# One program in five queues: the order of work and 89 engine choices drawn anew, in a kernel of a recurrent attention and a Fourier mixing block

## The chip, the cores and the metric

The kernel runs on one core of one Trainium2 chip. The core has a matrix engine (TensorE, PE in the profile; its weight loads are listed apart as PEld), a vector engine (VectorE, DVE), a scalar engine (ScalarE, ACT), GpSimd (POOL) and SyncE (SP). Each has a queue of its own that it works through in the order in which the program lists it. Data moves between main memory (DRAM) and on-chip memory (SBUF) by DMA. Matmul results land in PSUM, which the program uses as eight banks, each of 512 float32 values per partition.

The metric is the device time of one execution in microseconds (us), less is better. The times shown are medians over several executions.

## The reference

Inputs are r, k, v and w of shape batch 4 x heads 8 x sequence 768 x head size 48, u (8 x 48), and two weight matrices (384 x 1536 and 1536 x 384). First a linear attention with a decaying state:

```python
for t in range(S):
    cur = np.einsum('bhd,bhe->bhde', u[None] * kt, vt)
    y[:, :, t] = np.einsum('bhd,bhde->bhe', rt, state + cur)
    state = wt[:, :, :, None] * state + np.einsum('bhd,bhe->bhde', kt, vt)
```

Then, on x, which is y with its heads side by side (4 x 768 x 384):

```python
X = np.fft.fft(np.fft.fft(x, axis=1), axis=2)
u = x + np.real(X)
un = (u - mean) / np.sqrt(var + 1e-06)      # over the last axis
out = u + np.maximum(un @ w_ch1, 0.0) @ w_ch2
```

The output is float32, 4 x 768 x 384.

## The kernel before

*Tiling.* The four batches are cut into six chunks of 128 time steps each, chunk (b, c). Within a chunk the recurrence is written as matrix products: the logarithms of w are summed up along time by a matmul with a triangular matrix (lines 944 and 948), exponentials of the sums (lines 950 and 963) scale r and k (`rkh`, lines 982 and 985), both are transposed (`rkt`), their product gives a 128 x 128 matrix per head (line 1014) that is masked (line 1019) and multiplied with v (line 1064), and a state of 48 x 48 per head is carried from chunk to chunk (line 1040, its decay at 1048). The term with u is `rk`: r times k (967), times u (969), summed over a head (971), times v (`vtd`, 974). Batch 0 handles its chunks in pairs (`attention2`). For the first two batches the transposes of `rkt` run on TensorE; from chunk 12 on they are DMA transposes that SP issues (line 990).

*Mixing.* The rows of a batch are folded by symmetry (`sd`, `xf`), multiplied with cosine and sine tables (line 1128, results `hcs`, and a reversed copy of them, `hcr`, lines 1137 to 1142), then with a second table (line 1151). The sum with x is `uf` (1153), its statistics follow (1157, 1159), then the centred rows `un` (1163), which are transposed to `unt`, on TensorE for batches 0 and 1 and by DMA (line 1180) for batches 2 and 3. For each half batch (three chunks of 128 rows) twelve products with the first weight matrix (line 1198) are evicted with a ReLU to `ht`, on ACT (line 1205) or DVE (line 1203), and the products with the second one (line 1216) are scaled, added to `uf` on DVE (line 1220) and written out by a DMA that SP issues (line 1224).

*Order.* The program first makes a list of 1439 operations, numbered as they are made, each with its dependencies and the engines that could do it. The dictionary `ORDER` at the head of the file says for each of the five engines which operations it does, and in which order. So an operation that several engines can do runs on the engine under which its number stands. `_Prog.schedule` walks through these lists with fixed cost figures, in which it also decides which PSUM bank a tile gets (the one that is free first by its figures). `_Prog.emit` then writes the instructions and a semaphore wait wherever an operation needs a result of another engine. An engine that waits holds up everything behind it in its own list; SP's list holds all loads, outputs and DMA transposes, except for the two weight matrices, which POOL issues. Instructions whose operands allow more than one engine pass through helpers, so that many have the same line in the profile (533 for products and sums of two tensors, 547 and 556 for ACT, 557 for DVE copies).

*Numbers that the text uses.* The operations below belong to the last chunks of batch 3, its mixing and its last products.

| number | engine | what it does |
|---|---|---|
| 1203, 1202 | SP | load r and k of chunk (3, 4) |
| 1232, 1233 | SP | load k and r of chunk (3, 5) |
| 1011 | SP | DMA transpose of the second half of `un` of batch 2 |
| 1217, 1211, 1212, 1183 | POOL | k part of `rkh` of (3, 4); `rk` of (3, 4) and its product with u; `vtd` of (3, 3) |
| 1192, 1213 | DVE | decay of the state of (3, 3); head sums of `rk` of (3, 4) |
| 1245, 1246 | DVE | r part and k part of `rkh` of (3, 5) |
| 1247, 1248 | SP, PE | DMA transpose of `rkt` of (3, 5); its 128 x 128 products |
| 1336, 1338, ..., 1358 | PE | the twelve first products of half 0 of batch 3, each followed by the number of its eviction (1337, 1339, ...) |
| 1360 to 1407 | PE, DVE, SP | second products, evictions and outputs of batch 3 |
| 1080, 1085, 1090 | DVE | output evictions of half 1 of batch 2 |

Of the kernel before, what the change touches and what calls it, by code (L numbers as in the profile page):

```python
# [35 lines left out]
        "6 1419 1420 1421 1422 1423 1424 1425 86 92 1426 94 1427 1428 1429 78 1430 97 1431 82 113 115 146 1432 1433 "  # L36
        "148 1434 114 128 116 151 1435 1436 80 121 134 202 124 204 1437 167 169 425 1438 168 170 207 127 136 223 "
        "130 175 137 224 225 178 426 428 226 182 183 181 185 186 190 231 192 234 238 193 455 239 457 437 237 454 "
        "254 438 246 241 441 242 255 247 484 256 466 444 257 262 270 271 467 263 258 272 273 486 483 274 470 275 "
        "259 276 277 278 279 280 281 264 265 266 267 513 284 473 302 293 303 304 285 286 495 515 294 496 322 295 "  # L40
        "313 447 314 331 332 323 502 324 476 333 512 315 291 309 547 549 300 525 580 524 356 346 362 352 344 354 "
        "364 499 528 329 360 348 350 320 342 338 358 546 591 397 399 534 579 531 403 401 381 558 505 559 385 590 "
        "383 393 776 778 562 594 366 367 775 376 567 565 389 368 377 395 597 802 804 612 371 604 372 605 801 378 "
        "620 373 621 606 622 613 614 615 623 624 607 625 626 608 609 627 628 629 630 631 616 788 617 387 791 643 "
        "828 634 644 635 645 636 391 830 652 672 653 410 681 654 673 682 854 674 683 856 827 411 641 663 664 665 "
        "405 415 814 650 412 406 817 659 853 885 407 820 416 712 417 679 887 794 702 704 670 688 706 696 843 698 "
        "840 866 714 694 915 700 884 747 872 737 869 753 739 914 692 749 741 743 731 846 726 708 900 897 727 1098 "
        "710 1124 1097 902 926 1126 751 1100 716 936 745 929 944 937 728 733 1150 952 945 953 717 954 938 1152 718 "
        "955 956 946 939 940 957 958 959 960 941 961 947 1176 948 962 963 949 735 973 1123 980 974 721 975 966 967 "
        "981 982 1004 997 968 1005 1113 722 998 765 723 1178 1006 990 999 766 991 992 755 756 760 1110 1136 1139 "  # L50
        "757 767 761 1149 762 1175 1022 1020 1014 1036 1018 1028 1026 1116 1024 1016 1142 1030 1207 1165 1209 1038 "
        "1188 1162 1032 1039 1043 1206 1044 1034 1236 1194 1168 1237 1065 1191 1069 1059 1073 1045 1055 1219 1061 "
        "1053 1222 1048 1248 1224 1075 1057 1067 1274 1251 1040 1063 1049 1266 1071 1267 1275 1077 1258 1259 1276 "
        "1268 1277 1269 1260 1261 1278 1279 1262 1280 1263 1281 1282 1283 1270 1271 1284 1285 1082 1295 1288 1289 "
        "1290 1302 1296 1297 1326 1303 1312 1304 1319 1327 1087 1328 1078 1313 1320 1050 1321 1088 1314 1083 1079 "
        "1084 1089 1338 1342 1344 1350 1340 1348 1358 1354 1336 1356 1391 1389 1393 1377 1397 1387 1383 1346 1352 "
        "1381 1375 1370 1379 1371 1365 1399 1385 1360 1361 1362 1372 1366 1395 1367 1409 1414 1410 1404 1411 1400 "
        "1401 1415 1405 1416 1406"),
    "act": (
        "0 20 21 22 23 24 25 26 91 87 93 103 95 96 79 108 145 98 83 147 117 150 149 118 119 201 162 152 203 81 424 "  # L60
        "206 205 171 427 172 173 208 174 138 157 131 227 229 228 218 213 73 453 429 187 194 458 482 456 439 511 545 "
        "434 248 251 74 468 469 492 463 485 446 260 487 282 268 283 475 497 498 516 578 290 308 299 514 292 301 550 "
        "526 527 357 347 328 345 582 355 365 504 319 337 311 349 321 521 351 359 548 593 398 361 774 581 404 402 "
        "560 561 382 386 384 400 779 312 555 587 340 800 777 394 540 396 826 805 603 573 390 852 803 610 784 632 "
        "618 388 611 831 633 392 640 857 829 883 642 649 793 658 678 810 651 341 660 661 687 855 819 836 713 862 "
        "669 888 703 689 680 697 707 699 913 845 715 917 886 695 701 748 740 916 750 693 1096 742 893 871 738 744 "
        "690 732 754 1122 709 662 711 1127 922 752 878 1174 746 908 1101 1148 734 1099 935 942 964 1153 965 1125 "
        "736 1106 979 1132 986 972 1179 1115 1003 1158 1151 691 1177 1205 1023 1015 1021 1141 1029 1037 988 1010 "
        "1017 1019 1027 1210 1031 1184 1167 1033 989 1235 1208 1035 1238 1239 1012 1070 1066 1013 1060 1074 1193 "
        "1215 1062 1200 1056 1054 1244 1076 1058 1064 1072 1257 1230 1068 1264 1272 1273 1301 1332 1325 1341 1347 "  # L70
        "1380 1334 1310 1311 1384 1396 1394 1335"),
# [1221 lines left out]
```

## Time and profile before

| | us |
|---|---|
| median of the runs shown (181.91 to 183.27, three runs) | 181.93 |
| the profiled execution's own time | 181.62 |
| its span, from the first to the last instruction | 179.8 |
| time of the profiled execution outside the span | 1.82 |
| loads of one chunk and one input, issue to landing (median) | 3.8 to 4.5 |
| DMA transposes of `rkt`, issue to landing (median) | 3.4 |
| outputs, issue to landing (median) | 2.3 |

The profile page gives busy times of the engines, a picture of the span in 40 slices, the chain of work that ended last and groups of instructions by line. Further views answer questions: busy time by stretches, instructions in order of time, who waited for whom. A line such as `131.20 0.89 DVE L533 ... rkh<-in_k,e` reads: it started 131.20 us into the span, took 0.89 us, ran on DVE, stands at line 533 of the program, and wrote `rkh` from `in_k` and `e`; a bracket behind it says how long the engine stood idle ahead of it and what ended that.

The span holds 1776 matmuls. The packets of the DMA queues are small: 105,201 of 108,935 have under 512 bytes, as a head's row of 48 float32 values has 192.

### The profile page before, as it was taken

Reading aid. Unit: us, or ns where it says so; the run is one execution under the profiler, and the core shown is the slowest. Engines: PE = TensorE matmul, PEld = TensorE weight load, DVE = VectorE, ACT = ScalarE, POOL = GpSimd, SP = SyncE. Lnnn points to the kernel's source line nnn. Section 1 sums busy time; section 2 is a strip of 40 time slices with the busy share of each in tenths; the row PEclk is TensorE's granted clock in tenths of the full one; section 3 lists DMA queues with packets and bytes.
Section 4 is the critical chain, followed back from the end, with each engine's and each line's share of the span. In section 5 each row is a group of like instructions: output and inputs, shape, how many; then the busy total and the mean of one; then the engine's idle time right before and its main releaser. Section 6 shows DMA issues by size and latency. Waiting matters only on the chain.

```text
span 179.8 us, 4644 instructions
## 1 busy us (share of the span) xinstructions
PE 171.9 (96%) x1776; PEld 123.8 (69%) x1776; DVE 158.4 (88%) x376; ACT 121.3 (67%) x285; POOL 95.1 (53%) x118
## 2 busy tenths in 40 slices
PE   5989999999999999999999999999997999999993
PEld 2455677776888667668787776677775766887671
DVE  8998999999999989999897889999897989795443
ACT  4999999999999538799978863498775331304020
POOL 3146799599986727879539447591966030000000
PEclk9999999999999999999999999999999999999999
DMA  5999999899989989797999999798996004402133
GB/s 150 322 325 258 185 237 180 170 179 198 161 170 210 215 165 203 165 252 115 216 204 229 185 218 193 152 186 163 192 161 178 0 4 103 116 0 108 70 142 121
DMA packets 108935, 30.58 MB, mean 170 GB/s; under 512 B 105201, under 2 KB 108402, under 8 KB 108786
## 3 DMA queue, kind: packets, MB, share of 16 engines
q1 hardware_dynamic: 108370, 27.93, 72.7%
q0 software_dynamic: 544, 2.36, 7.1%
q8 instruction: 14, 0.23, 0.5%
q14 instruction: 7, 0.06, 0.1%
HBM read 23.59 MB, written 4.72 MB: 157 GB/s over the span
## 4 chain that ended last, share of the span: by engine, by line
PE 79%; DVE 6%; ACT 6%; DMA 5%; SPq 1%; issue 1%; ACTq 0%; DVEq 0%
PE bank L1198 24%; PE bank L1216 23%; PE bank L1151 5%; PE bank L1128 4%; PE bank L1014 3%; DMA rkt<-rkh 3%; DMA in_k<-in_k_dram 2%; PE bank L948 2%; PE bank L1064 2%; PE bank L913 1%; PE bank L839 1%; PE bank L944 1%; PE bank L1061 1%; PE bank L862 1%; PE bank L1040 1%; PE bank L1174 1%
## 5 line engine op out<-in xcount | busy, mean ns | idle before, releaser
L1198 PE MATMUL bank<-unt,w 128*128 128x384 bf16 x288 | 54.6, 328 | 0.0
L1216 PE MATMUL bank<-w,ht 128*128 128x384 bf16 (+2 forms) x300 | 54.0, 319 | 0.0
L1205 ACT ACTIVATE ht<-bank 128x384 bf16<-128x384 f32 x73 | 33.4, 497 | 22.7 <-PE bank L1198 21.9
L1198 PEld LDWEIGHTS bank<-unt,w 128*128 128x128 bf16 x288 | 39.0, 144 | 6.0 <-DMA unt<-un 0.2
L1216 PEld LDWEIGHTS bank<-w,ht 128*128 128x128 bf16 x300 | 27.8, 98 | 15.4 <-DVE ht L1203 0.2
L1019 DVE TENSOR_TENSOR ah<-bank,msk 128x512 bf16<-128x512 f32 x36 | 23.2, 680 | 2.0 <-PE bank L1014 1.9
L533 POOL TENSOR_TENSOR rk<-rk,ub 128x384 f32<-128x384 f32 x18 | 18.0, 1005 | 9.8 <-DVE rk L533 8.4
L533 POOL TENSOR_TENSOR vtd<-in_v,dc 128x384 f32<-128x384 f32 (+1 forms) x22 | 18.2, 832 | 6.7 <-DVE bank L1048 2.9
L533 POOL TENSOR_TENSOR rk<-in_r,in_k 128x384 f32<-128x384 f32 x16 | 16.3, 1020 | 9.9 <-DVE xf L533 7.8
L533 POOL TENSOR_TENSOR rkh<-in_k,e 128x384 bf16<-128x384 f32 x18 | 18.0, 1003 | 5.5 <-ACT e L963 4.8
L547 ACT ACTIVATE un<-uf,agg 128x384 bf16<-128x384 f32 x20 | 11.8, 617 | 12.9 <-DVE agg L1159 12.8
L1220 DVE SCALAR_TENSOR_TENSOR osb<-bank,rstd,uf 128x384 f32<-128x384 f32 (+2 forms) x25 | 14.7, 595 | 5.2 <-PE bank L1216 5.2
L1203 DVE TENSOR_SCALAR ht<-bank 128x384 bf16<-128x384 f32 x23 | 11.7, 552 | 4.3 <-PE bank L1198 4.2
L547 ACT ACTIVATE vb<-in_v 128x384 bf16<-128x384 f32 x24 | 12.1, 519 | 2.7 <-DMA in_v<-in_v_dram 2.7
L1153 DVE TENSOR_TENSOR uf<-bank,x 128x384 f32<-128x384 f32 x24 | 12.4, 547 | 0.9 <-PE bank L1151 0.8
L1157 DVE BATCH_NORM_STATS2 bst<-uf 128x6 f32<-128x384 f32 x24 | 12.5, 547 | 0.0
L547 ACT ACTIVATE lb<-in_w 128x384 bf16<-128x384 f32 (+1 forms) x21 | 12.0, 575 | 0.7 <-DMA in_w<-in_w_dram 0.5
L556 ACT ACTIVATE rkt<-bank 128x512 bf16<-128x512 bf16 x20 | 12.1, 652 | 0.1
L1070 DVE TENSOR_TENSOR x<-bank,vtd 128x384 f32<-128x384 f32 x18 | 9.7, 552 | 1.9 <-PE bank L1064 1.9
L982 DVE TENSOR_TENSOR rkh<-bank,in_r 128x384 bf16<-128x384 f32 x18 | 9.9, 550 | 1.5 <-ACT bank L950 1.5
L963 ACT ACTIVATE e<-bank 128x392 f32<-128x392 f32 (+1 forms) x18 | 8.9, 493 | 2.0 <-PE bank L957 1.4
L1151 PE MATMUL bank<-dtm,hcr 128*128 128x384 bf16 x36 | 9.6, 326 | 0.1
(167 smaller groups left out, 344.8 us busy)
## 6 DMA issues: line engine op xcount, KB each, us to landing
out_dram<-osb SPq DMA_DIRECT2D x23, 192.0 KB, 2.3
in_w<-in_w_dram SPq DMA_DIRECT2D x18, 192.0 KB, 4.5
in_k<-in_k_dram SPq DMA_DIRECT2D x18, 192.0 KB, 3.9
in_r<-in_r_dram SPq DMA_DIRECT2D x18, 192.0 KB, 3.8
in_v<-in_v_dram SPq DMA_DIRECT2D x18, 192.0 KB, 3.8
w<-in_moe_w_ch_dram POOLq DMA_DIRECT2D x2, 1152.0 KB, 9.9
in_r<-in_r_dram SPq DMA_DIRECT2D x3, 384.0 KB, 4.9
in_k<-in_k_dram SPq DMA_DIRECT2D x3, 384.0 KB, 4.9
```

The costliest lines, as they stand in the source:

```text
L533: return lambda e: e.tensor_tensor(out=o, in0=a, in1=b, op=f)
L547: return lambda e: e.activation(o, a, f, **kw)
L556: {"act": lambda e: e.activation(o(), i(), ACTF.Copy), "dve": lambda e: e.tensor_copy(out=o(), in_=i())}, **kw)
L1019: masked[n] = op("dve", v_1(512), lambda e, x=x: e.tensor_tensor(out=ah[:, x:H:2, :], in0=ps(ta[x])[:, :].rearrange("p (h t) -> p h t", t= ...
L1151: return e.matmul(ps(t)[:, 0:DM], (hcs if kb < NP else HCR)[:, j, a:a + 128], DTM[:, j, :], start=(j == 0), stop=(j == 2))
L1153: op("dve", v_1(DM), lambda e, kb=kb, t=t: e.tensor_tensor(out=uf[:, kb, :], in0=ps(t)[:, 0:DM], in1=xb[:, kb, 0:DM], op=ALU.add), r=[t, ( ...
L1157: op("dve", v_1(DM), lambda e, kb=kb, bs=bs: e.bn_stats(bs[:, :], uf[:, kb, :]), r=[("UF", i, kb)], w=[("BST", n % 4)])
L1198: ins = e.matmul(ps(t)[:, 0:384], W1[:, m, j:HID:NJ], unt[:, :, m, :], start=(m == 0), stop=(m == NM - 1))
L1203: {"dve": lambda e, j=j, t=t, ht=ht: e.tensor_scalar(out=ht[:, j, :], in0=ps(t)[:, 0:384], scalar1=-1.0, scalar2=0.0, op0=ALU.mult, op1=AL ...
L1205: "act": lambda e, j=j, t=t, ht=ht: e.activation(ht[:, j, :], ps(t)[:, 0:384], ACTF.Relu, scale=-1.0)},
L1216: ins = e.matmul(ps(t)[:, 0:hi - lo], ht[:, j, 128 * x:128 * x + 128], W2[:, j, lo:hi], start=(j == 0), stop=(j == NJ - 1))
L1220: op("dve", v_1(hi - lo) + 64, lambda e, kb=kb, t=t, o=o, lo=lo, hi=hi: e.scalar_tensor_tensor(out=o[:, lo:hi], in0=ps(t)[:, 0:hi - lo], s ...
```

## The change

The five lists of `ORDER` are replaced; nothing else in the file differs. The operations, their dependencies and the numbers of instructions stay. 89 operations stand under another engine: 28 move from DVE to ACT, 24 from ACT to DVE, 20 from DVE to POOL, 14 from POOL to DVE and 3 from POOL to ACT. PE and SP keep their 538 and 126 operations; ACT goes from 285 to 292, DVE from 376 to 366, POOL from 114 to 117. By kind, the largest groups are the ReLU evictions `ht` (17 from DVE to ACT, 8 from ACT to DVE), the evictions of the transposes `rkt` and `unt` (10 from ACT to DVE, 6 from DVE to ACT), the products and sums of line 533 between DVE and POOL, and the reversed copies `hcr`, four of which leave POOL and one of which comes. In the last batch twelve `ht` evictions go from DVE to ACT.

Most operations shift by a few places in their list. In SP's list the load of w (84) now comes first of all. The load 1203 goes from ahead of 1161 to just ahead of 1011; from 1011 to 1309 the list is as it was. In the cut below, the first lines of SP's list, the lines of all engines that hold the last chunk, and the last stage are kept.

```diff
-        "1188 1162 1032 1039 1043 1206 1044 1034 1236 1194 1168 1237 1065 1191 1069 1059 1073 1045 1055 1219 1061 "
-        "1053 1222 1048 1248 1224 1075 1057 1067 1274 1251 1040 1063 1049 1266 1071 1267 1275 1077 1258 1259 1276 "
...
+        "1162 1188 1038 1043 1039 1236 1206 1044 1237 1191 1168 1194 1030 1053 1069 1073 1059 1061 1065 1219 1045 "
+        "1055 1274 1275 1222 1048 1248 1224 1067 1057 1075 1266 1267 1251 1063 1040 1071 1049 1258 1259 1268 1276 "
...
-        "1084 1089 1338 1342 1344 1350 1340 1348 1358 1354 1336 1356 1391 1389 1393 1377 1397 1387 1383 1346 1352 "
...
+        "1079 1084 1338 1350 1348 1340 1336 1342 1352 1356 1354 1344 1346 1358 1370 1391 1395 1371 1377 1365 1389 "
...
-        "1215 1062 1200 1056 1054 1244 1076 1058 1064 1072 1257 1230 1068 1264 1272 1273 1301 1332 1325 1341 1347 "
-        "1380 1334 1310 1311 1384 1396 1394 1335"),
...
+        "1068 1058 1076 1230 1072 1064 1257 1264 1286 1273 1265 1301 1308 1339 1332 1337 1353 1310 1311 1357 1341 "
+        "1349 1334 1359 1351 1347 1378 1335 1376 1380 1390 1394 1384 1398 1392 1396"),
...
-        "1190 1216 1195 1169 1245 1246 1197 1198 1192 1213 1220 1221 1223 1242 1250 1249 1225 1226 1252 1227 1253 "
...
+        "1182 1189 1216 1192 1195 1169 1213 1245 1246 1197 1240 1062 1220 1221 1223 1242 1249 1225 1250 1226 1227 "
+        "1252 1229 1253 1228 1254 1255 1256 1041 1272 1046 1291 1298 1305 1299 1306 1300 1292 1307 1293 1294 1322 "
+        "1051 1329 1330 1323 1315 1331 1316 1324 1325 1080 1317 1318 1343 1090 1085 1345 1355 1388 1368 1373 1382 "
...
-        "877 892 876 904 906 1102 951 1134 1128 1154 1186 1105 1160 1155 1129 1180 1181 1131 1183 1157 1217 1211 "
-        "1212 1196 1240 1241 1199 1214 1243 1265 1287"),
...
+        "892 874 875 877 921 876 904 934 1102 943 1128 1134 1129 1103 1154 1155 1160 1186 1157 1105 1180 1131 1181 "
+        "1217 1211 1183 1212 1196 1198 1241 1214 1199 1243 1287"),
...
-        "89 88 85 84 90 141 143 142 199 198 197 144 420 449 421 422 450 478 481 200 507 452 451 423 541 479 480 574 "
...
-        "1095 1145 1121 1120 1146 1119 1147 1171 1109 1135 730 1172 987 725 1201 720 1203 1161 1187 1173 1202 1231 "
-        "1011 1233 1232 1218 1204 1247 1234 769 759 764 1309 1042 1047 1333 1052 1091 1081 1086 1374 1364 1369 1413 "
...
+        "84 88 85 89 90 143 141 142 198 199 197 449 420 423 144 479 478 421 422 200 481 541 452 450 480 451 574 508 "
...
+        "1119 1171 1120 1095 1121 414 1109 1145 1135 1147 1172 987 725 1201 720 1173 730 1161 1187 1231 1202 1203 "
+        "1011 1233 1232 1218 1204 1247 1234 769 759 764 1309 1052 1042 1047 1333 1081 1086 1091 1374 1369 1364 1413 "
```

98 rows, old and new, of the table ORDER are left out of this document.

## The prediction

> **What bounds the kernel now.** I read the page from the top, then busy time by stretches of the span, then the chain of work that ended last. First the page: span, busy time, and the sharing of the DMA engines in 40 slices.
>
> ```profile
> span 179.8 us, 4644 instructions
> ## 1 busy us (share of the span) xinstructions
> PE 171.9 (96%) x1776; PEld 123.8 (69%) x1776; DVE 158.4 (88%) x376; ACT 121.3 (67%) x285; POOL 95.1 (53%) x118
> ...
> DMA  5999999899989989797999999798996004402133
> ```
>
> TensorE is busy for 96% of the span, and the DMA engines are at 90% or more in most slices up to three quarters of it. The busy time by stretches says where the 7.9 us without a matmul lie. Columns: stretch, its length, then busy time and instruction count of PE, PEld, DVE, ACT and POOL, the granted clock, the DMA share and GB/s.
>
> ```profile
> 0.00:33.00 33.00, 29.64 (x448) 18.74 (x449) 31.35 (x101) 29.58 (x60) 19.95 (x37) 1.00 0.99 236
> 33.00:66.00 33.00, 32.79 (x366) 25.27 (x364) 32.09 (x74) 29.09 (x69) 25.90 (x30) 1.00 0.97 184
> 66.00:100.00 34.00, 33.94 (x346) 25.23 (x344) 31.63 (x68) 28.35 (x72) 23.77 (x25) 1.00 0.96 194
> 100.00:135.00 35.00, 35.00 (x329) 25.16 (x328) 32.05 (x69) 23.74 (x60) 20.82 (x22) 1.00 0.99 181
> 135.00:153.00 18.00, 16.81 (x141) 11.58 (x139) 16.02 (x38) 6.17 (x16) 4.68 (x6) 1.00 0.29 74
> 153.00:179.80 26.80, 23.74 (x158) 17.82 (x156) 15.23 (x30) 4.41 (x12) 0.00 (x0) 1.00 0.28 92
> ```
>
> From 33 to 135 us PE lacks 0.27 us of 102 (32.79 + 33.94 + 35.00 against 33 + 34 + 35): nothing to win there, as long as the order keeps PE fed. The gaps are the start (33.00 - 29.64 = 3.36), one in 135 to 153 (18.00 - 16.81 = 1.19), and the end. The DMA engines are full until 135 (0.96 to 0.99) and then fall to 0.29: in that time PE and DMA both run at their limit, and whatever is last in the DMA queue decides when the final 43 us begin. The chain shows it (start, us, what; it skips short pieces):
>
> ```profile
> 6.33 1.29 ACT L707
> 7.73 0.85 ACT lb L547
> ...
> 125.35 1.42 SPq L1180
> 126.81 0.72 SPq L596
> 127.58 3.53 DMA in_k<-in_k_dram
> 131.20 0.89 DVE rkh L533
> 132.12 4.60 DMA rkt<-rkh
> 136.81 0.40 PE bank L1014 x8
> ...
> 170.86 5.89 PE bank L1216 x48
> 176.85 0.62 DVE osb L1220
> ```
>
> The last chunk of the last batch is loaded (in_k), multiplied on DVE (operation 1246 of the order, line 985), transposed by DMA (1247, line 990), and PE waits for it (1248, line 1014). After 136.81 PE has work to 176.85, and the last eviction and output take the rest, 2.95 us. PE's own view has the wait in brackets:
>
> ```profile
> 136.81 0.40 PE L1014 MATMUL bank<-rkt 48*128 48x128 bf16 x8 [1.19 <-DMA rkt<-rkh]
> ```
>
> So PE stood ready at 135.62. This is the only gap of size behind the start, and the place where a new order of the queues can show one for one.
>
> **The change part by part.** PE keeps its 538 operations; 89 of the others change engine (28 DVE to ACT, 24 ACT to DVE, 20 DVE to POOL, 14 POOL to DVE, 3 POOL to ACT), and all five queues are permuted, by a median of 1 (SP) to 4 places.
>
> *The start.* ACT's table load ends at 7.62 and its first logarithm begins at 7.73 (rows above). The order of ACT up to there is unchanged, and the load of w, moved to the head of SP's queue, comes earlier than the 7.73 at which ACT is free to use it. DVE's sine arguments change places among each other; the sum of what stands ahead of the last one is the same to one memset. Cost 0. If that is wrong, everything behind 6.33 moves by the difference. The most that the start could give is its 3.36 us of PE idle time, of which the waits give 2.0 to the first matmul:
>
> ```profile
> PE bank L1237 <- POOL osb L607: 2.0, 1, 2.0
> ```
>
> It needs a GpSimd iota that moves up by one place only, so of the 3.36 about 1.4 are in reach.
>
> *Engine swaps, 33 to 135 us.* The clearest change of price is the reversed copy of the mixing result (lines 1137 to 1142), three of which leave POOL for ACT:
>
> ```profile
> L1138 ACT ACTIVATE hcr<-hcs,cp x3: 592/605/617, 38.1 to 106.4; 128x384 bf16<-128x384 bf16 x3
> L537 POOL TENSOR_SCALAR hcr<-hcs x3: 1170/1182/1196, 40.1 to 107.0; 128x384 bf16<-128x384 bf16 x3
> ```
>
> That is 1.18 against about 0.6 us each, three times, so 1.7 us of latency; but PE waits for none of it (0.27 us lost in 102). All swaps of this stretch cost and give 0, and the work that hides them is PE's own queue. If that cover fails, one swap costs the difference of two rows, at most 0.6 us. DVE, at 32.09 of 33 the tightest, gets lighter on balance (14 POOL and 24 ACT operations come, 48 leave). Of the reordered DMAs each takes SP about 0.6 us, and a load that is moved ahead pushes the others back by that.
>
> *The last chunk.* Here the order of three queues changes around the chain. On POOL and DVE before:
>
> ```profile
> 126.05 1.62 POOL L533 TENSOR_TENSOR vtd<-in_v,dc 128x384 f32<-128x384 f32 x2 [2.93 <-DVE bank L1048]
> 127.63 1.00 POOL L533 TENSOR_TENSOR rkh<-in_k,e 128x384 bf16<-128x384 f32 x1
> 128.59 1.03 POOL L533 TENSOR_TENSOR rk<-in_r,in_k 128x384 f32<-128x384 f32 x1
> 129.69 1.01 POOL L533 TENSOR_TENSOR rk<-rk,ub 128x384 f32<-128x384 f32 x1
> 130.66 1.02 POOL L533 TENSOR_TENSOR sd<-x 128x385 f32<-128x385 f32 x1
> ```
>
> ```profile
> 129.53 1.02 DVE L1070 TENSOR_TENSOR x<-bank,vtd 128x384 f32<-128x384 f32 x2 [0.45 <-PE bank L1064]
> 130.47 0.55 DVE L982 TENSOR_TENSOR rkh<-bank,in_r 128x384 bf16<-128x384 f32 x1
> 131.20 0.89 DVE L533 TENSOR_TENSOR rkh<-in_k,e 128x384 bf16<-128x384 f32 x1 [0.18 <-DMA in_k<-in_k_dram]
> ```
>
> In the new order DVE has two operations more ahead of 130.47: a state decay (1192), which fits into the idle 0.45 ahead of 129.53, and the reduction 1213, which stands directly ahead of it and waits for POOL's rk<-rk,ub (1212). That one now stands behind a vtd product (1183, half of the 1.62, 0.81), and the first rk product (1211) needs a load of r (1203) that SP now issues five places later, right ahead of the transposition of un (1011). SP before:
>
> ```profile
> 122.20 0.64 SPq L596 DMA_DIRECT2D in_k<-in_k_dram  x1
> 122.89 2.05 SPq L596 DMA_DIRECT2D in_w<-in_w_dram  x1
> 125.06 1.71 SPq L1180 DMA_TRANSPOSE unt<-un  x1
> ```
>
> The same DMAs stand ahead of 1011 in both orders, so it goes out at about 125.06 again. The load of r leaves as the last of them, between 122.9 and 124.5 (2.05 or a usual 0.6 us of issue ahead of 125.06), and lands 3.53 later like in_k: 126.4 to 128.0. POOL's rkh can start at 125.8 (in_k, 122.20 + 3.53) instead of 127.63, as the two vtd products no longer stand ahead of it. Then rk 126.8 to 128.0 at its start, 1.03, vtd 0.81, and rk<-rk,ub 1.01: its end is 129.7 to 130.9. DVE's reduction starts at 130.47 (the x row's end) to 130.9, takes about 0.47 to the next start, as these rows follow each other (129.53, two of them, 130.47), the next product the same: 1246 starts at 131.41 to 131.84 against 131.20. Its duration is bounded by 0.55 (its neighbour) and its own 0.89: end 131.96 to 132.73 against 132.09, so -0.1 to +0.6. I take +0.3, the middle. SP's issue, the 4.60 of the transposition and PE's wait follow it one for one: +0.3 on the span. If the wait vanished altogether, -1.19; if POOL got no head start (rk<-rk,ub ending 0.81 later than its 130.70, at 131.5), 1246 would end at 133.3, +1.2.
>
> On those 0.89 a rule of the Trainium skill bears: SBUF — State Buffer, section "SBUF: two separate sides", says that a DVE operation with two SBUF inputs and a GpSimd one that reads SBUF hold one shared port exclusively, and the later one is blocked for the whole of the earlier. The trace agrees: POOL's sd ends at 131.68, and 131.68 plus 0.41 is 132.09, the end of 1246. By the rule the 0.34 above 0.55 go if the new order parts the two and stay if sd again runs beside it; both are inside the two ends above.
>
> *The end.* Twelve of the last batch's 24 ReLU evictions go from DVE to ACT:
>
> ```profile
> L1203 DVE TENSOR_SCALAR ht<-bank x18: 548/548/559, 154.3 to 172.2; 128x384 bf16<-128x384 f32 x18
> L1205 ACT ACTIVATE ht<-bank x6: 472/491/491, 155.8 to 171.3; 128x384 bf16<-128x384 f32 x6
> ```
>
> ACT then has 18 x 0.49 = 8.8 us of them where it had 6 x 0.49 = 2.9 of its 4.41, DVE 6 x 0.55 = 3.3 where it had 9.9 of its 15.23. In 26.80 us both have room, and before 176.85 PE has no idle time to win: 0. The last three outputs end as before, with 1406 last on PE and 1407 behind it.
>
> *Sum:* the profiled execution took 181.62, 1.82 more than its span of 179.8. 181.62 + 0 + 0 + 0.3 + 0 = 181.9. The median of the runs shown, 181.93, is 0.31 above the profiled one, so the forecast of the median is 181.93 + 0.3 = **182.2 us**.
>
> **Rivals.** (1) *The wait for the last chunk goes.* For it: POOL's idle 2.93 ahead of 126.05 shows a queue that was held by its order, and the un products that gate 1011 now stand on ACT ahead of where DVE did the last of them. Against: DVE's new reduction. It saves up to 1.19: 180.7. With the reachable 1.4 of the start added it would be 179.3; only with a good part of that is it faster by over 1% (below 180.1), which is also about what a measurement of this kernel can tell from no change.
>
> (2) *The last ReLU stage runs out of PSUM banks* (slower). In the new order the second, third and fourth tiles that PE fills from 153 us on (operations 1350, 1348, 1340) are evicted by ACT only after the eighth (ACT's order 1339, 1332, 1337, 1353, 1310, 1311, 1357, 1341, 1349, ..., 1351), and on DVE two output evictions of the batch before stand behind the first ReLU (1343, 1090, 1085). I count 2 such outputs and 6 ReLU tiles undrained when PE wants the ninth: eight banks, none spare. As long as DVE reaches 1343 when its matmul ends, nothing is lost; from the point where its three output evictions (1080, 1090, 1085, 0.62 each as in the chain's last row) and that ReLU (0.55) run behind PE, PE stops for up to 1.86 + 0.55 = 2.4 us: 184.3. For: 153 to 177 has no idle PE today and so no slack in it. Against: DVE loses 12 x 0.55 = 6.6 us of work there. The Trainium skill, Perfetto Trace Analysis, section "Matmuls", has the general rule: rotate through the banks so that one eviction overlaps the next matmuls; no row of before shows what eight full banks cost.
>
> (3) *It changes nothing:* PE is fed as before and the 1.19 stay: 181.9, inside the forecast's own range.
>
> **How the numbers follow.** Forecast together with (3): 0.52, own range 181.5 to 183.1 (-0.4 to +1.2 around 181.93). Rival 1: 0.27, of which 0.13 are beyond 1% faster. Rival 2 with its 184.3, or another wait of that size: 0.21, slower by over 1% (above 183.75). So faster 0.13, same 0.66, slower 0.21. The range reaches into both rivals: 180.3 (1.6 below the median, the 1.19 and 0.4 of the start) to 184.3.
>
> **What would show it.** Right: PE still over 99% busy from 33 to 135; the wait of line 1014 for the transposed chunk still there, 0.8 to 2.4 us, with the reduction of line 971 directly ahead of the last two rkh products on DVE, and 1246 ending 0 to 1.2 us later against the span's start; no PE gap behind 153. Rival 1 shows as that wait gone and 1014's last run starting by 135.6; rival 2 as idle PE at line 1198 between 153 and 160, released by ACT or DVE ht. Wrong altogether would be a PE gap that none of the steps names, say at the first use of the second weight matrix (line 1216, near 58 us), whose load POOL now issues behind other products, or a start that is longer by the time of a late memset.

## The result, and the profile after

| | before | after |
|---|---|---|
| median of 20 executions each, us | 182.32 | 182.12 |
| lowest to highest, us | 181.47 to 183.66 | 179.75 to 186.00 |
| profiled execution, its span, us | 181.62, 179.8 | 181.42, 179.5 |

The ratio of the new kernel to the old one is 0.9942, with a 95% interval of 0.9915 to 0.9969. It leaves out executions more than 1.5% above a kernel's fastest, seven of the new kernel's twenty and none of the old one's, which takes away the upper end of the new kernel's wider scatter; so it shows more of a gain than the medians of all executions (182.12 / 182.32 = 0.9989). The forecast was 182.2 us, slightly slower than before; the new kernel is level or slightly faster.

Busy time of the new kernel by stretches, with the columns explained in the prediction:

```profile
0.00:33.00 33.00, 27.32 (x433) 17.43 (x434) 31.06 (x102) 28.41 (x58) 19.05 (x33) 1.00 0.96 228
33.00:66.00 33.00, 32.78 (x369) 25.26 (x367) 31.38 (x71) 29.40 (x72) 28.11 (x35) 1.00 0.98 185
66.00:100.00 34.00, 34.00 (x347) 25.30 (x346) 31.68 (x70) 27.31 (x68) 24.68 (x27) 1.00 1.01 196
100.00:135.00 35.00, 35.00 (x331) 25.31 (x329) 32.73 (x71) 22.62 (x58) 21.13 (x23) 1.00 0.99 181
135.00:153.00 18.00, 18.00 (x152) 12.54 (x151) 16.11 (x36) 7.51 (x18) 4.96 (x6) 1.00 0.34 90
153.00:179.50 26.50, 23.40 (x156) 17.67 (x154) 10.27 (x23) 8.92 (x23) 0.00 (x0) 1.00 0.27 87
```

Two stretches differ. From 135 to 153 us PE now has no gap (18.00 busy; it had 16.81), and in the first 33 us it is busy 2.32 us less (27.32 against 29.64; 1.0 of that is the twenty filler matmuls of line 1259, which take 4.74 in place of 5.75 us, so it is not all loss). To set the two executions side by side I subtracted, for every PE operation, the undisturbed time of all operations ahead of it in its list from its start. By this measure PE in the new kernel is level at 30 us, about 0.8 us behind at 32 and about 1.0 behind from there to 132, and 0.3 ahead from 138 on. So the new order **loses about one microsecond near 30 us and gets back more than that at the last chunk.**

*The loss.* POOL from 25 to 31 us, first in the new kernel, then in the one before:

```profile
25.19 0.99 POOL L533 TENSOR_TENSOR rk<-rk,ub 128x384 f32<-128x384 f32 x1
27.19 0.83 POOL L533 TENSOR_TENSOR vtd<-in_v,dc 128x384 bf16<-128x384 f32 x1 [1.01 <-DVE dc L819]
27.97 1.14 POOL L533 TENSOR_TENSOR xf<-x 128x191 bf16<-128x191 f32 x2
```

```profile
25.18 1.00 POOL L533 TENSOR_TENSOR rk<-rk,ub 128x384 f32<-128x384 f32 x1
26.13 1.15 POOL L533 TENSOR_TENSOR xf<-x 128x192 bf16<-128x192 f32 x2
27.23 1.62 POOL L533 TENSOR_TENSOR vtd<-in_v,dc 128x384 bf16<-128x384 f32 x2
```

In the old order the two `xf` products (operations 140 and 132) fill the time in which `vtd` (212) waits for a sum from DVE. In the new order `vtd` stands ahead of them, POOL is idle for 1.01 us, and both `xf` come 1.8 us later. PE of the new kernel waits for them and for what follows on POOL; these two waits are not in the kernel before:

```profile
29.17 0.34 PE L1128 MATMUL bank<-cs,xf 128*128 128x386 bf16 x1 [0.66 <-POOL xf L533]
31.00 0.38 PE L1004 MATMUL bank<-idw,rkh 128*128 128x128 bf16 x4 [0.62 <-POOL rkh L533]
```

*The gain.* DVE's product (1246) comes 1.44 us later than before, and yet PE does not wait. DVE and PE of the new kernel:

```profile
132.64 0.55 DVE L533 TENSOR_TENSOR rkh<-in_k,e 128x384 bf16<-128x384 f32 x1
...
136.62 0.40 PE L1014 MATMUL bank<-rkt 48*128 48x128 bf16 x8
```

The reason is the DMA transposition between them (1247). Here is the DMA view of the stretch in which its packets move, first before (133.3 to 136.1 us), then after (134.4 to 135.9):

```profile
q1 hardware_dynamic: 1233, 0.30, 115.2%
q8 instruction: 1, 0.02, 2.7%
...
rkt<-rkh SPq DMA_TRANSPOSE x1, 4.6
```

```profile
q1 hardware_dynamic: 1100, 0.27, 95.5%
...
rkt<-rkh SPq DMA_TRANSPOSE x1, 3.1
```

It took 4.6 us before and takes 3.1 now. Before, one packet of the queue that the profile calls "instruction" stood among the transposition's. That packet has 16,384 bytes and ran from 133.95 to 135.16 us. Of the transposition's 1024 packets 966 had started by 134.68; the last 58, a little under a sixteenth, started only from 135.15 on, as the large packet ended. In the new kernel the large packet runs at 137.89, and all 1024 start between 134.40 and 135.85. There are 14 such packets in an execution. Their number times 16,384 bytes is about 64 bytes for each of the some 3,600 instructions of PE (matmuls and weight loads), so I take them for PE's program; the trace does not say so.

### The profile page after: what moved, and what is told of

It reads as the page before. It is cut to its first block, busy times and chain, and to the rows that moved or that the text cites. A ratio compares the mean times of both kernels' runs of the same rounds, so it can differ in the third digit from the quotient of the medians.

```text
span 179.5 us, 4637 instructions
## 1 busy us (share of the span) xinstructions
PE 170.5 (95%) x1776; PEld 123.5 (69%) x1776; DVE 153.2 (85%) x366; ACT 124.2 (69%) x292; POOL 97.9 (55%) x121
## 4 chain that ended last, share of the span: by engine, by line
PE 80%; ACT 9%; DVE 6%; POOL 2%; issue 1%; DVEq 0%; ACTq 0%; POOLq 0%
PE bank L1198 27%; PE bank L1216 26%; PE bank L1151 5%; PE bank L1128 4%; PE bank L1014 3%; PE bank L1064 2%; PE bank L1061 2%; ACT rkt L556 1%; PE bank L944 1%; PE bank L1174 1%; PE bank L948 1%; PE bank L1040 1%; ACT lb L547 1%; ACT hcs L556 1%; ACT bank L794 1%
## 5 line engine op out<-in xcount | busy, mean ns | idle before, releaser
L1198 PE MATMUL bank<-unt,w 128*128 128x384 bf16 x288 | 54.0, 328 | 0.1
L1205 ACT ACTIVATE ht<-bank 128x384 bf16<-128x384 f32 x82 | 37.6, 504 | 18.7 <-PE bank L1198 18.5
L533 POOL TENSOR_TENSOR rkh<-in_k,e 128x384 bf16<-128x384 f32 x19 | 18.9, 1001 | 13.1 <-ACT st L556 6.0
L533 POOL TENSOR_TENSOR rk<-rk,ub 128x384 f32<-128x384 f32 x21 | 21.0, 1004 | 3.2 <-DVE rk L533 2.6
L533 POOL TENSOR_TENSOR vtd<-in_v,dc 128x384 f32<-128x384 f32 (+1 forms) x23 | 19.0, 831 | 3.6 <-DVE dc L971 1.7
L533 POOL TENSOR_TENSOR xf<-sd 128x382 bf16<-128x382 f32 (+1 forms) x8 | 8.0, 1005 | 11.5 <-DVE xf L533 6.5
L1203 DVE TENSOR_SCALAR ht<-bank 128x384 bf16<-128x384 f32 x14 | 7.5, 552 | 6.8 <-PE bank L1198 6.8
L950 ACT ACTIVATE bank<-bank 128x384 f32<-128x384 f32 x18 | 8.9, 497 | 6.1 <-PE bank L944 6.0
L547 ACT ACTIVATE vb<-in_v 128x384 bf16<-128x384 f32 x22 | 11.4, 532 | 1.6 <-DMA in_v<-in_v_dram 1.6
```

The source lines that it names most:

```text
L533: return lambda e: e.tensor_tensor(out=o, in0=a, in1=b, op=f)
L547: return lambda e: e.activation(o, a, f, **kw)
L1198: ins = e.matmul(ps(t)[:, 0:384], W1[:, m, j:HID:NJ], unt[:, :, m, :], start=(m == 0), stop=(m == NM - 1))
L1205: "act": lambda e, j=j, t=t, ht=ht: e.activation(ht[:, j, :], ps(t)[:, 0:384], ACTF.Relu, scale=-1.0)},
```

## The experiments

The theory (D in the expectations) is: early loss on POOL, late gain because the large packet no longer hits the last transposition. Its rivals: the order of the last chunk's queues makes the gain (Q); early changes are absorbed (A). "The kernel before" was run beside all of them; each ratio is to its runs on the same chip. Kernels joined from the two orders keep each operation on the engine of the part that it comes from. In three kernels (POOL's products put back, and two joined ones) the program is four lines shorter, so their L1010 is line 1014.

**POOL's two products put back.** On the new kernel:

```diff
-222 215 212 140 132 217 436
+222 215 140 132 212 217 436
```

> The new kernel with one edit: on POOL the two xf operations 140 and 132 stand ahead of the vtd 212 again, as in the kernel before. Theory D (delay early, collision late): the new order loses about 1.0 us of PE between 28 and 32 us, because vtd waits for a DVE reduction with the two xf behind it (PE waits 0.66 ahead of 29.17 and 0.62 ahead of 31.00). Then both waits go, PE runs 0.6 to 1.0 us earlier from 32 us on, and as PE alone sets the end of the new kernel, the time falls by most of that: ratio to the kernel before 0.987 to 0.991. Rival A (the delay is absorbed): the wait for the last transposed chunk at line 1014 comes back with 0.5 to 1.0 us, and the ratio stays that of the new kernel, 0.992 to 0.997.

Measured: 181.56 us (before 182.64), ratio 0.9948 (0.9919 to 0.9978). The two early waits fall from 0.66 and 0.62 us to 0.27 and 0.16, and PE is 0.5 us less behind than in the new kernel at 33 us and 0.6 at 100, but only 0.2 at 110 and at 130. And the profiled execution (182.51, among the slowest of this kernel) has the large packet at 134.92, in the transposition, and its wait:

```profile
137.80 0.40 PE L1010 MATMUL bank<-rkt 48*128 48x128 bf16 x8 [1.36 <-DMA rkt<-rkh]
```

PE's list is that of the new kernel, whose packet ran at 137.89. So the list alone does not fix the packet's place. The expected gain did not show, and the run left the question to the ones below.

**Twelve matmuls more at the start of the kernel before,** to move the packet:

```diff
-            return e.matmul(ps(tw)[:, 0:384], MSK[:, :], IDW[:, :])
+            for j in range(3 if i < 6 else 1):
+                lo, hi = (128 * j, 128 * j + 128) if i < 6 else (0, 384)
+                ins = e.matmul(ps(tw)[:, lo:hi], MSK[:, :], IDW[:, lo:hi])
+            return ins
```

> The kernel before with the first six filler matmuls of the start cut into three of 128 columns each: 12 matmuls more, the same columns, nothing else. In the kernel before a packet of 16,384 bytes of the DMA queue called instruction (133.95 to 135.16 us) fell into the transposition of the last chunk's rkt (packets 133.30 to 134.68, the last 58 of 1024 only from 135.15 to 136.01), which took 4.60 us instead of some 3.2. Theory D: the packet follows PE's instruction count, so it comes about 1 us earlier, the transposition takes 3.2 to 3.8 us, PE's wait at line 1014 falls from 1.19 to 0 to 0.5, ratio 0.993 to 0.997. Rival Q (the wait is the work of the order in the queues of the last chunk, not of the packet): wait 1.0 to 1.3, ratio 0.999 to 1.002.

Measured: 182.67 (182.64), ratio 0.9997 (0.9972 to 1.0021). The packet did not move (134.25, inside), the transposition took 5.2 us, the wait was 1.41. The edit was too small, so it tells nothing between the theories.

**The start of the kernel before, the rest of the new one** (cut at 40 us; POOL's list around the cut, against the new kernel):

```diff
-195 196 252 250 245 431 66 488 261 494 459 523 460 433 517 557
+188 139 133 195 196 244 252 431 494 261 65 459 488 523 460 433 517 557
```

> All that the kernel before started by 40 us in its order and on its engines, all the rest in the order and on the engines of the new one. Theory D: the early loss of 1.0 us is gone, and the end is that of the new kernel: ratio 0.987 to 0.991, no PE gap over 0.5 us from 20 to 40 us. Rival A: the wait at line 1014 comes back, ratio 0.992 to 0.997. A third theory, S: the scatter of the new kernel (179.75 to 186.0) comes from its start; then these runs lie within 1.5 us of each other.

Measured: 182.93 (182.64), ratio 1.0013 (0.9978 to 1.0048), 182.03 to 185.10. The expected ratio was lower, and the scatter stays, so it does not come from the first 40 us alone. The early waits are gone, but PE is 0.5 us behind the kernel before at 40 us, 0.9 at 45 and 1.4 at 80: it waits 0.51 and 0.25 us for ACT's `un` at 43.07 and 44.17 us, behind the seam, where neither kernel waits. A joined order has costs of its own, and this run cannot be read for one part. Two other runs with the old order there (the new end, the later load) are also 0.5 us behind at 40 us, so that much between two profiles can be scatter. The packet runs at 137.98, outside, the transposition takes 3.1 us, there is no wait, and PE makes up 1.2 us at the last chunk.

**The kernel before up to 112 us, the new one behind it** (SP's list against the kernel before):

```diff
-1201 720 1203 1161 1187 1173 1202 1231 1011 1233
+1201 720 1173 1161 1187 1231 1202 1203 1011 1233
```

> All that the kernel before started by 112 us as there, the rest (last chunk, last stage) as in the new kernel. Theory D: PE comes to the last chunk as early as in the kernel before (135.6) and the transposition ends by then or 0.5 later, as the packet of the queue called instruction falls elsewhere: wait at line 1014 0 to 0.5, ratio 0.992 to 0.996. Rival Q gives the same if the order of the queues is better, but with the transposition at 3.2 us and 1246 ending earlier than 132.09; if the new order of the last chunk's queues only costs (forecast of the prediction), 1246 ends 0.3 to 1.1 later than 132.09 and the ratio is 0.998 to 1.003.

Measured: 181.53 (182.64), ratio 0.9931 (0.9898 to 0.9963). **With the new order behind 112 us alone, the whole gain is there.** The packet runs at 138.24, outside, the transposition takes 3.1 us, there is no wait. 1246 ends at 133.53, 1.4 later than before, but this execution had lost 1.2 us at 45 us already (below), and the transposition's 1.5 us less make up for it.

**The reverse: the new kernel up to 112 us, the one before behind it** (SP's list against the new kernel):

```diff
-1201 720 1173 730 1161 1187 1231 1202 1203 1011 1233
+1201 720 1203 1161 1187 1173 1202 1231 1011 1233
```

> All that the new kernel started by 112 us as there, the rest as in the kernel before. Theory D: the early loss of 1.0 us reaches the end, since the last chunk's loads and products follow PE, and the wait at line 1014 is there with 0.8 to 1.4: ratio 1.002 to 1.006. Rival A (the wait takes the loss in): ratio 0.999 to 1.001, with a wait of 0.1 to 0.5. Rival F (the gain was made before 112 us): 0.992 to 0.997.

Measured: 183.89 (182.74), ratio 1.0063 (1.0029 to 1.0097). PE is 1.2 us behind the kernel before at 110 us, as in the new kernel, but 3.2 at 130, because it waits behind the seam where neither kernel waits: 0.59 us for ACT ahead of 117.50 us, and twice more:

```profile
120.77 0.34 PE L944 MATMUL bank<-lb,msk 128*128 128x384 bf16 x1 [0.34 <-DVE ah L1019]
128.22 0.62 PE L1014 MATMUL bank<-rkt 48*128 48x128 bf16 x16 [0.48 <-DMA rkt<-rkh]
```

So the 0.6% is the price of the first 112 us and of the seam together, and the two are not separated. The packet is inside again (136.75), the transposition takes 4.6 us, and PE waits 0.78 us for it although it comes later (the profile names ACT's `ht`, but that had ended 0.7 us earlier): the loads and products of the last chunk come later with it. That speaks against A. The product of this ratio and the one before it, 0.9931 x 1.0063 = 0.9994, is above the 0.9942 that the same measure gives for the whole change, with intervals that overlap; so the two runs do not show what each part is worth.

**The last stage alone** (cut at 139 us; ACT's list against the kernel before):

```diff
-1264 1272 1273 1301 1332 1325 1341 1347 1380 1334 1310 1311 1384 1396 1394 1335
+1264 1286 1273 1265 1301 1308 1339 1332 1337 1353 1310 1311 1357 1341 1349 1334 1359 1351 1347 1378 1335
...
```

> All that the kernel before started by 139 us as there, the rest (the twelve ReLU evictions on ACT, the order of the last products) as in the new kernel. Theory D and the prediction: the last stage has no idle PE time and gives 0: ratio 0.999 to 1.001, wait at line 1014 1.0 to 1.4. Rival E (the lighter DVE of the last stage makes the gain): 0.992 to 0.997. The prediction's second rival (banks full): 1.005 to 1.013, with idle PE at line 1198 from 153 to 160.

Measured: 182.58 (182.74), ratio 1.0018 (0.9995 to 1.0041). The twelve evictions on ACT neither gain nor cost, and no bank runs out. From 153 us on PE runs without a gap in this kernel, and the wait ahead of it is the old one:

```profile
153.78 6.01 PE L1198 MATMUL bank<-unt,w 128*128 128x384 bf16 x36
```

```profile
137.44 0.40 PE L1014 MATMUL bank<-rkt 48*128 48x128 bf16 x8 [1.28 <-DMA rkt<-rkh]
```

**The packet moved far, order untouched.** On the kernel before, sixty matmuls more:

```diff
-            return e.matmul(ps(tw)[:, 0:384], MSK[:, :], IDW[:, :])
+            for j in range(4):
+                ins = e.matmul(ps(tw)[:, 96 * j:96 * j + 96], MSK[:, :], IDW[:, 96 * j:96 * j + 96])
+            return ins
```

> The kernel before with all twenty filler matmuls of the start cut into four of 96 columns each: 60 matmuls more (120 instructions on PE, about half of what lies between two packets of 16,384 bytes of the DMA queue called instruction), the same columns, nothing else. The 12 matmuls more of the run before it had left the packet where it was (134.25 us). Theory D (the wait of the last chunk is made by that packet): it comes at 128 to 132 or at 138 to 142, the transposition of the last rkt takes 3.1 to 3.6 us, PE's wait at line 1014 falls to 0 to 0.4, ratio 0.993 to 0.996. Rival Q (the order in the queues makes the wait): transposition or its issue later by other causes, wait 1.0 to 1.4, ratio 0.999 to 1.002.

Measured: 181.82 (182.74), ratio 0.9969 (0.9937 to 1.0000). The packets run at 131.79 and 141.63, the transposition takes 3.7 us and PE does not wait for it, with every queue in the old order. The expected ratio was lower. The profiled execution was about 1.0 us behind the kernel before at 12 us already, and again at 35; its granted clock was 0.991, and whether the edit or the clock cost that is not separated.

**The packet moved into the new kernel's transposition,** by the same edit on the first thirteen fillers:

```diff
+            for j in range(4 if i < 13 else 1):
+                lo, hi = (96 * j, 96 * j + 96) if i < 13 else (0, 384)
...
```

> The new kernel with the first thirteen filler matmuls of the start cut into four of 96 columns each: 39 matmuls more (78 instructions), which should bring the packet of the queue called instruction from 137.9 us to about 135, into the transposition of the last rkt (134.4 to 135.9). Theory D: the transposition takes 4.2 to 4.7 us where the packet falls into it, PE waits 0.8 to 1.4 at line 1014, ratio to the kernel before 0.998 to 1.002. Rival Q: ratio as of the new kernel, 0.992 to 0.997, and no wait.

Measured: 182.49 (182.74), ratio 0.9968 (0.9930 to 1.0007), 180.62 to 184.46. The profiled execution has the packet at 131.96, so it missed the target there, and no wait. Inconclusive.

**A cheaper way to move the packet: 108 instructions more,** on three kernels. Only matmuls of the first 8 us are cut:

```diff
-        for i in range(NE):
-            ins = e.matmul(ps(tw)[:, 0:384], CI.bitcast(BF16)[:, 0:128], CI.bitcast(BF16)[:, 0:384])
+        for i in range(4 * NE):
+            j = 96 * (i % 4)
+            ins = e.matmul(ps(tw)[:, j:j + 96], CI.bitcast(BF16)[:, 0:128], CI.bitcast(BF16)[:, j:j + 96])
...
+            for j in range(4 if i < 7 else 1):
...
```

On the old kernel with the new order behind 112 us:

> The run that was as the kernel before up to 112 us and as the new kernel behind it, with 108 more instructions on PE: the eleven matmuls of the start and the first seven fillers cut into four of 96 columns each. That kernel's times fell into two groups, 180.5 to 181.3 and 181.7 to 182.7. Theory D: the upper group is the packet of the queue called instruction falling into the last transposition in some executions; with the packet 4 to 6 us away the upper group is gone, median 180.5 to 181.2, ratio 0.988 to 0.992. Rival W: the upper group is the 1.07 us that PE waits at 45.5 us (its profiled execution had it) for DVE's rkh product, whose r load left SP 0.7 us later than in the kernel before and met the load of the first weight matrix; then both groups stay, ratio 0.992 to 0.995.

Measured: 181.08 (182.51), ratio 0.9938 (0.9915 to 0.9962); packets at 129.80 and 142.54, no wait for the transposition. The median is as D expected, the ratio as W did; five of twelve executions still lie above 181.4. So the packet is not all of the upper group. The profiled execution does not have the wait at 45 us.

On the new kernel with POOL's two products put back:

> The new kernel with POOL's two xf operations ahead of vtd again, and the 108 more instructions on PE. Theory D: no wait at line 1014, the early loss of 1.0 us down to 0.3, and so at least 0.4 us less than the new kernel: median 180.5 to 181.2, ratio 0.988 to 0.992. Rival A (what PE gains early is lost again, because the loads of the last chunks are bound by the DMA engines): ratio 0.993 to 0.996, with 1203 and 1232 issued within 0.3 us of the new kernel's 123.50 and 128.34.

Measured: 180.84 (182.51), ratio 0.9922 (0.9892 to 0.9952), **the fastest kernel of the study** by its median, though its interval overlaps those of the next ones. The median is as D expected and the ratio just above D's range. Packets at 129.35 and 144.74, the transposition 3.4 us, no wait at line 1014; PE is 0.3 us behind the kernel before at 130 us and 0.9 ahead from 138. The load 1203 leaves SP at 123.59 us and 1232 at 127.47, 0.1 later and 0.9 earlier than in the new kernel, so the loads are not held as A had it. POOL is no longer idle in front of `vtd`:

```profile
25.97 1.14 POOL L533 TENSOR_TENSOR xf<-x 128x191 bf16<-128x191 f32 x2
27.07 1.62 POOL L533 TENSOR_TENSOR vtd<-in_v,dc 128x384 bf16<-128x384 f32 x2
```

On the kernel before, order untouched:

> The kernel before, its order untouched, with the 108 more instructions on PE (the eleven matmuls of the start and the first seven fillers cut into four of 96 columns each). Theory D in its strong form: the packet alone makes the wait and the order of the last chunk's queues gives nothing; then the packet comes near 130 and near 142 us, the wait at line 1014 is 0 to 0.3, and the time is that of the same edit on the kernel with the new order behind 112 us: median 181.0 to 181.3, ratio 0.992 to 0.995. Rival Q: the new order of the last chunk gives part of it; then this one stays between, ratio 0.996 to 0.999, with a wait of 0.4 or more.

Measured: 182.08 (182.99), ratio 0.9967 (0.9938 to 0.9996). The wait is gone, as D says, but the time stays between, as Q says. PE of this kernel, and the DMA view from 134.6 to 136.5 us, in which the transposition's packets move:

```profile
119.53 3.63 PE L1198 MATMUL bank<-unt,w 128*128 128x384 bf16 x21 [0.41 <-DMA unt<-un]
...
134.46 0.40 PE L1014 MATMUL bank<-rkt 48*128 48x128 bf16 x8
136.38 0.34 PE L1040 MATMUL bank<-vb,rkh 128*128 128x96 bf16 x4 [0.39 <-ACT vb L547]
137.30 0.40 PE L1014 MATMUL bank<-rkt 48*128 48x128 bf16 x8
```

```profile
q1 hardware_dynamic: 1626, 0.37, 116.3%
...
rkt<-rkh SPq DMA_TRANSPOSE x1, 3.5
```

Line 1014 runs without a wait for `rkt`. But another large packet now runs at 117.45 us, and PE waits 0.41 for a transposition of `un` behind it; the run with sixty matmuls had a packet at 118.29 and 0.21 in the same place. Moving the packets moves the hits. The traces suggest why the time stays between: this profile is 0.6 us behind the kernel before at 110 us and 1.2 behind from 121 on, after that wait, and makes up 0.8 at the last chunk. The joined kernel with the same edit, whose lists are the same up to 112 us, is level up to 130 and makes up 0.7 there. So what these two profiles differ by, 1.0 us, arose ahead of the last chunk and not in the order of its queues.

**A load that leaves SP 0.7 us later.** The profiled execution of the kernel joined at 112 us had lost 1.2 us at 45 us, where its order is still the old one. DVE's product 522 had started at 44.88 in place of 43.54. Its load of r (509) had left SP by 34.48, in the kernel before by 33.75. To bring that about, in SP's list of the kernel before:

```diff
-574 508 509 510 575 542
+574 508 575 509 510 542
```

> The kernel before with one edit in SP's list: the load of k of chunk (0, 4) (575) stands ahead of the loads of r and v of chunk (0, 2) (509, 510) in place of behind them. So in_r leaves SP about 0.7 us later and meets the packets of the first weight matrix (on the DMA engines from 35.8 to 43.9 us). Theory W: it lands some 10 us after its issue in place of 5 and more, DVE's rkh product (operation 522) starts 1 us later or more, PE waits 1.0 to 1.5 us at line 998 near 45 us, and since the last chunk follows PE the time rises by most of it: ratio 1.003 to 1.007. If the weight load is not what delays the r load: DVE's product at 43.5 as before, ratio 0.999 to 1.001.

Measured: 183.62 (182.51), ratio 1.0055 (1.0024 to 1.0085). DVE and PE:

```profile
44.97 0.56 DVE L982 TENSOR_TENSOR rkh<-bank,in_r 128x384 bf16<-128x384 f32 x1 [0.86 <-DMA in_r<-in_r_dram]
```

```profile
45.67 0.38 PE L998 MATMUL bank<-idw,rkh 128*128 128x128 bf16 x4 [0.87 <-DVE rkh L982]
```

The four r loads of 28 to 47 us, issue to landing (least, median, most), first before, then here:

```profile
DMA to landing us min/median/max: 4.8/5.2/5.4
```

```profile
DMA to landing us min/median/max: 4.8/5.4/10.8
```

The load left SP at 34.12 to 34.78 and took 10.8 us. The 384 packets of 3,072 bytes of the first weight matrix occupy the DMA engines from 36.1 to 44.2 us here, from 35.8 to 43.9 before; that they are what delays the load is read from these times. The load that left by 33.75 got past them, the one that left 1.0 us later did not, and the whole program ended a microsecond later. As the joined kernel had the same wait without this edit, in a stretch where its order is the old one, it can also come by itself: a second source of scatter beside the packet. That the new kernel has it is not shown; the r loads of that stretch landed within 5.1 us in its profile.

*All fourteen profiles together.* In six the packet lies inside the last transposition: before, and the runs with POOL's products put back, with twelve matmuls, with the new start, with the new end, and with the later load. There the transposition takes 4.5 to 5.2 us, and PE waits 0.78 to 1.41 us at line 1014. In the other eight it lies outside; the transposition takes 3.1 to 3.7 us, and PE's matmuls never wait for it. Set against the kernel before, PE makes up 0.7 to 1.3 us between 130 and 145 us in those eight, and loses 0.5 to gains 0.3 in the other five with a hit. Two of the eight have the old order at the last chunk (108 instructions, sixty matmuls more), and make up 0.8 and 0.9.

The other transpositions point the same way. The fourteen profiles hold 224 of them. 103 had no packet of 8,192 or 16,384 bytes of an instruction queue on the way between issue and landing, and took 3.0 to 4.5 us, median 3.2. 121 had one, and took 3.1 to 6.5, median 4.0; all 44 above 4.5 us are among them. So a meeting does not always cost, and part of the difference is that a longer transfer is likelier to meet a packet.

## Why the prediction was wrong

*The range and the size.* 182.1 lies inside 180.3 to 184.3, and "same" was the likeliest case. The sign was wrong, and the sum came out near by luck, because two errors cancel: about +1.0 near 30 us where I had 0, and the whole wait of 1.19 gone where I had it stay and grow by 0.3.

*The last chunk: the step that failed.* I wrote that "SP's issue, the 4.60 of the transposition and PE's wait follow it one for one". The first half held in size, but not by my path. 1246 ended at 133.19, 1.10 later than before, of which 1.0 is PE's lateness from the early loss; the new order of DVE and POOL cost about 0.1, inside my -0.1 to +0.6. POOL's head start did not come: I had its `rkh` start at 125.8, as soon as `in_k` was there.

```profile
127.91 1.00 POOL L533 TENSOR_TENSOR rkh<-in_k,e 128x384 bf16<-128x384 f32 x1 [6.03 <-ACT st L556]
...
130.62 1.01 POOL L533 TENSOR_TENSOR rk<-rk,ub 128x384 f32<-128x384 f32 x1
```

POOL's sum for the reduction ended at 131.63 (130.62 + 1.01), 0.93 later than before. That cost nothing only because DVE's `x` row ahead of the reduction, late with PE, ended at 131.80.

But **the 4.60 is not the price of that transposition**; it is 3.1 and a hit by the instruction packet (1.5 us). The table in front of the prediction gives a median of 3.4 for these transpositions, and the row with 4.60 stood 1.2 above it. I took the odd duration as given, where the question was what made it odd; the answer stood in the DMA view of those 2.8 us. With 3.1 in place of 4.60 the sum for the last chunk would have been a wait that goes (1246's end of 132.09 + 0.3, and 3.1, is 135.5, ahead of PE's 135.62), which is rival 1, reached on a path that I had not seen.

*Order and engine swaps ahead of the last chunk.* I had put the start and the swaps at 0, the swaps as hidden by PE's own queue. That failed at one place in POOL's list, for 1.0 us. I had looked at the start (before 8 us) and at 33 us and later, and the loss lies between, at 28 to 32. The 1.0 us is read from the traces; the times do not resolve it (0.9942 with it, 0.9931 with the old order up to 112 us, 0.9948 with the two products put back). My sign held in its letter (PE busy 101.78 of 102 us from 33 to 135) and missed it. I had bounded a failed cover by the duration of one swapped operation, 0.6; here an operation with a wait moved past two that others need, and the price is the wait.

*The end.* 0 was right: the run with the last stage alone gives 1.0018 with an interval that holds 1, and rival 2 (full banks) did not happen.

*The 0.89 us of 1246.* The Trainium skill, SBUF — State Buffer, section "SBUF: two separate sides", says that such a DVE operation is blocked while GpSimd's holds the shared port. In the new kernel POOL's `sd` is over just before it:

```profile
131.59 1.01 POOL L533 TENSOR_TENSOR sd<-x 128x385 f32<-128x385 f32 x1
```

It ends at 132.60 (131.59 + 1.01), 1246 starts at 132.64 and takes 0.55 in place of 0.89. The trace agrees with the rule: the two are parted, and the 0.34 are gone. So do the others: in the six profiles in which 1246 starts while `sd` runs (before, and the runs with twelve and sixty matmuls, the new start, the new end and the later load) it takes 0.65 to 1.17 us and ends 0.40 to 0.42 us behind `sd` each time.

*The late transposition.* Why a blocked sixteenth would delay all of it: DMA: Bandwidth & Descriptors, section "Why a DMA increments its semaphore by 16 and not by 1", of the Trainium skill says that a DMA runs on up to 16 engines and is complete only when each has finished its share. The 58 late packets of the kernel before, against 64 for a sixteenth, agree with that. The other hits are not all of this form: behind the gap stood 28, 86 and 141 packets in three of them, but 418 and 525 in two (the runs with twelve matmuls and with the later load). So one blocked sixteenth is a reading of the first trace, which does not name the engines; that the whole transposition ends late behind the packet is what all six show.

*Still open.* What sets the packet's place: it differs by 3 us between the new kernel and the one with POOL's products put back, which have the same PE list, and no kernel was profiled twice. How much of the late 0.7% is the packet: the joined order with the packet moved away gives 0.9938, the old order with it moved away 0.9967, and their intervals overlap; by the traces the old order without a hit makes up 0.8 to 0.9 us, the new one 0.7 to 1.3, so a part for the new order of the last chunk is possible and not shown. And how much of the new kernel's scatter is hits: its four longest executions (183.93 to 186.00) ran at a granted clock of 0.981, the other sixteen at 0.990 to 1.000, so these four go with a lower clock; of the rest nothing is shown.

## What to carry to other kernels

Where a duration in the chain of work is far from the median of its kind, do not carry it into the sum; look in the DMA view of just that stretch for what shares the engines with it, the packets of the instruction queue included. In a queue that runs in order, price a moved operation by the wait that it brings along and by who stands behind it, not by the difference of two durations. And where the DMA engines are full, a load's price is set by what it leaves just ahead of or just behind.

## What the runs showed of the hardware

A packet of 16,384 bytes of the queue called instruction occupies its share of the DMA for 0.9 to 1.7 us, and the last transposition lands 1 to 2 us late where it is hit (4.5 to 5.2 us in place of 3.1 to 3.7, fourteen profiles). No transposition without an instruction packet on its way took more than 4.5 us (103 of 224). A meeting can cost less: in the run that missed its target, the packet at 131.96 stood in the transposition ahead of the last, which took 3.8. Its place moves with the number of instructions on PE only roughly: 24 instructions more left it where it was (134.25 against 133.95), 78, 108 and 120 more brought it to 129 to 132 us, and with one and the same PE list it ran at 134.92 in one kernel and at 137.89 in another. SP's issue of one load took 4.65 to 6.57 us in all fourteen profiles while the first weight matrix was on the DMA engines (36.50 to 43.07 in the new kernel), against a median of 0.8 to 0.9 for all its issues from 12 to 135 us; every load behind it waited. A DVE product with two inputs in SBUF that starts while POOL's `sd` runs ends 0.40 to 0.42 us behind it, six times of six.
